# Maxima of an attention unit: four bursts of two pairs, or three bursts of 3, 2 and 3 over two-bank tiles, and VectorE's ramp order written out

## The chip, the cores and the metric

The kernel runs on one core of a Trainium2 chip. The metric is the time of one execution on the device in microseconds; the median of three runs before the change is 1043.43 us. TensorE (PE) with its weight loads (PEld), VectorE (DVE), ScalarE (ACT) and GpSimd (POOL) each work through their own queue in order; SyncE (SP) issues most DMAs, in order too.

## The reference

```python
xn = _layernorm(x)                                   # x: 1 x 2048 x 640
q, k, v = split(xn @ wqkv)                           # 32 heads of 20
scores = q @ k^T * 20 ** -0.5, masked to 0 <= i - j < 256
o = softmax(scores) @ v @ wo
h = gelu(xn @ w_gate) * (xn @ w_up)                  # 1728 wide
return x + o + h @ w_down
```

All is float32, and softmax subtracts each row's maximum.

## The kernel before

**Products.** Dense products are made of three passes over a high and a low half of each operand (`dense_steps`): `ps_d` for q, k, gate and up, `ps_v` for v. The normalized input, transposed, is held as `xh` and `xl` in four chunks of 512 tokens (`C`).

**Three stages.** The *ramp* (to about 88 us) loads x by tiles of 128 tokens (`xi`), normalizes them (`ln_stats`, `ln_sqrt`, `ln_rstd`, `ln_apply`), transposes them on PE (`ps_t`), splits them (`xh` on ScalarE, `xl` on VectorE) and makes the first projections. Then `attention()` runs to about 541 us. After it come the remaining gate and up products (`ps_g`) and the products with `w_down` and `wo` (`ps`); the change leaves both alone.

**Attention** works in units: one group of 4 heads and one chunk of 512 queries, 8 groups by 4 chunks, 32 units. Each unit's loop has 14 slots (`NS`). What a slot does is written in the order in which each engine shall run it: PE, ACT, DVE, POOL and SP all take the order of the code there. In a slot come, one after the other:
- what was put off to this slot (`at`, `defer`, run by `tick`), with `max_end` last;
- maxima for the *next* unit (`pull_max`, `max_pair`), in some slots;
- in slot 0 the products of the last unit's `P` with v (`av_unit`: `ps_o`, 96 matmuls, 64 for a first chunk; then the copies `ob` and `P` on ACT, and three slots later `ob + P` on POOL, `ob` L630);
- in odd slots up to 11 two score pieces and their exponentials (`exp_piece`: `ps_e`, `P`);
- what was kept for the slot's end (`late`, `flush`), and loads of `qs` and `ks` for the unit after the next two (`load_stack`, slots 9 and 12);
- some 2.2 matmuls of dense work, the *fill* (`pull_fill(RATE / NS)`): projections and gate and up products that don't depend on the unit.

**The maxima.** A unit has 8 *pairs*. One pair is 128 queries of two heads: PE writes the scores of 320 keys into two PSUM tiles (`ps_m`, one for each half of PE's rows) with matmuls of 64 by 64 that use the four quadrants of the array side by side (L512), and VectorE adds the mask and takes the maximum of each tile in one reduction (`junk`, L522), which a second instruction reads out into `mx`. After the eighth pair two small VectorE instructions (`negate`, L531 and L532) make the negated maxima `nm` in two bf16 parts, `late`, at the slot's end. `max_end` transposes them on PE (`ps_n`, L539), copies them (`mr`, ACT) and sends them by DMA into two rows of `qs`, from where the score pieces of the next unit subtract them. `max_end` comes `MXD` = 7 slots after the eighth pair.

A *burst* is the pairs of one `pull_max`. Before, bursts of two pairs stand in slots 0 (ahead of `av_unit`), 0 again (behind it; in slot 3 of the first unit), 5 and 9. PSUM's 8 banks are two for `ps_d`, `ps_v` (`psd`), two for `ps_e`, `ps_o` (`psx`) and four tiles of one bank each for `ps_m`, `ps_n` (`psm`), which are used in turn.

**Beside it.** POOL clears what the mask hides in `P` (L592, L595), subtracts the low halves of weights (`wql`, L661), of projections (`pt`, L259), and in slots 0 to 2 of units 2 to 28 makes sums of `x` (`tx`, L758) for the last stage. `save_qk` moves a projection out in three steps; `LAG` says how many slots ScalarE's second step comes after VectorE's.

Of the kernel before, what the change touches and what calls it, by code (L numbers as in the profile page):

```python
# [9 lines left out]
F32 = mybir.dt.float32  # L10
# [10 lines left out]
NC = S // C  # L21
# [46 lines left out]
def block_kernel(ctx, tc, x, wqk, wv, wgu, wdo, wdl, out):  # L68
# [71 lines left out]
    psm = pp.enter_context(tc.tile_pool(name="psm", bufs=4, space=PSUM))  # L140

    def ln_load(t, lp):
        xi = lp.tile([128, D], F32, name="xi", tag="xi", bufs=8)
# [24 lines left out]
    def ln_apply(xi, mv, rs):  # L168
        nc.vector.tensor_scalar(xi, xi, mv[:, 0:1], rs, op0=OP.subtract, op1=OP.mult)  # L169

    def ln_scale(xs, lp, mv=None, begun=0):
        n = len(xs)
        mv = mv or lp.tile([128, n, 2], F32, name="mv4", tag="mv4", bufs=2)
        for i in range(begun, n):
            ln_stats(xs[i], mv[:, i, :], lp)
        rs = ln_rstd(*ln_sqrt(mv, n, lp), n, lp)
        for i, xi in enumerate(xs):
            ln_apply(xi, mv[:, i, :], rs[:, i:i + 1])

    def turn(k, xs, where):  # L180
        n = len(xs)
        pool, tag = {"x": (psx, "ex"), "m": (psm, "mx"), "o": (psm, "mx")}[where]
        ps = pool.tile([128, n * 128], F32, name="ps_t", tag=tag)
        for i in range(n):
            nc.tensor.transpose(ps[:, i * 128:(i + 1) * 128], xs[i][:, k * 128:(k + 1) * 128], ident)  # L185
        return ps

    def ln_turn(t0, xs, where="xmxmx"):
        n = len(xs)
        cs = slice(t0 * 128, (t0 + n) * 128)  # L190
        for k in range(KT):
            ps = turn(k, xs, where[k])
            nc.scalar.activation(xh[:, k, cs], ps, AF.Copy)
            nc.vector.tensor_tensor(out=xl[:, k, cs], in0=ps, in1=xh[:, k, cs].bitcast(F32), op=OP.subtract)  # L194

    acts = {}
    done = set()
# [27 lines left out]
    def behind(fn, *a):  # L225
# [3 lines left out]
        else:  # L229
            fn(*a)  # L230

    def load_qk(t):
        raw = wrp.tile([128, KT, 128], F32, name="wr", tag="wr")
        nc.sync.dma_start(raw, wqk[t])
        return raw

    def split_qk(raw):
        return split(wp, raw, [128, KT, 128], "wq", nc.gpsimd)
# [106 lines left out]
    def first_chunk(xs, wr0, wr5, prep, v0, lp):  # L345
# [26 lines left out]
        with tc.manual_schedule(engines=MANUAL | {mybir.EngineType.Pool}):  # L372
# [53 lines left out]
                    pass  # L426
            for j in range(4):
                ln_apply(xs[4 + j], mv[:, j, :], rs[:, j:j + 1])
            save_qk(0, 0, dn[0])
            mv = lp.tile([128, 4, 2], F32, name="mv4", tag="mv4", bufs=2)  # L430
            for j in range(2):
                ln_stats(xs[8 + j], mv[:, j, :], lp)
        save_qk(5, 0, dn[1])
        return w0, w5, v0, mv

    v0 = []
    with tc.tile_pool(name="lp", bufs=1, side="right") as lp:
        xs = [ln_load(t, lp) for t in range(2)]
        wr0 = load_qk(0)
        xs += [ln_load(t, lp) for t in (2, 3)]  # L440
        wr5 = load_qk(5)
        warm = lp.tile([128, 256], BF, name="warm")[:, 0:128]
        nc.vector.memset(warm, 0.0)
        ps = psd.tile([128, C], F32, name="ps_u", tag="dn")
        for i, n in enumerate(WARM):
            if i:
# [6 lines left out]
        w0, w5, v0, mv = first_chunk(xs, wr0, wr5, prep, v0, lp)  # L453
        ones = lp.tile([4, 2 * C], BF, name="ones")
        nc.gpsimd.memset(ones, 0.0)
        nc.gpsimd.memset(ones[0:2], 1.0)
        for i in range(NK):
            for j in (0, 2):
                nc.sync.dma_start(ks[i][SR:64, j:j + 2].rearrange("p j t -> p (j t)"), ones)
        for c in range(1, NC):  # L460
            if c > 1:
                ln_scale(xs[4 * c:4 * c + 4], lp, *((mv, 2) if c == 2 else ()))
            ln_turn(4 * c, xs[4 * c:4 * c + 4], "xmxmx" if c == NC - 1 else "xmxmm")
            if 1 < c < NC - 1:
                xs += [ln_load(t, lp) for t in range(4 * c + 4, 4 * c + 8)]
            if c == 1:
                for i in range(NQ):
                    for j in (0, 2):
                        nc.sync.dma_start(qs[i][SR + 2:64, j:j + 2].rearrange("p j t -> p (j t)"), ones[2:4])
            if c == 2:  # L470
                raws1 = [load_qk(1), load_qk(6)]
            if c < NC - 1:
                run(*[proj_v(v0, 4 * c - 4 + i, None if i % 2 else (psm, "mx")) for i in range(0 if c > 1 else 2, 4)])
                run(proj_qk(0, w0, c), proj_qk(5, w5, c))
# [15 lines left out]

    maxes = {}

    def max_pair(u, i):
# [5 lines left out]
        pss = [psm.tile([128, 320], F32, name="ps_m", tag="mx") for _ in range(2)]  # L499
        n = 320 if c else min(320, 128 * b + 128)  # L500

        def quarters(cut):
            for h in range(2):
                part = cut(128 * b + 64 * h - 256, 128 * b + 64 * h + 64)
                for r, ps in enumerate(pss):
                    if part is not None:
                        kt, col, k0, k1 = part
                        rows, j = slice(64 * r, 64 * r + SR), 2 * r + jj
                        q0 = 128 * b + 64 * h
                        ks_ = kt[rows, j, 0:1].to_broadcast([SR, 64]) if k0 == k1 else kt[rows, j, k0:k1]  # L510
                        w = max(64, k1 - k0) if k0 == k1 else k1 - k0
                        nc.tensor.matmul(ps[64 * h:64 * h + 64, col:col + w], q[rows, j, q0:q0 + 64], ks_,  # L512
                                         start=True, stop=True, tile_position=(64 * r, 64 * h))
# [5 lines left out]
        quarters(lambda lo, hi: (k, max(0, -lo), max(0, lo), hi))  # L519
        junk = ap.tile([128, 320], BF, name="junk", tag="junk", bufs=1)  # L520
        for r, ps in enumerate(pss):
            nc.vector.tensor_tensor_reduce(out=junk[:, 0:n], in0=ps[:, 320 - n:320], in1=mask[:, 320 - n:320], scale=1.0,  # L522
                                           scalar=NEG, op0=OP.add, op1=OP.max,
                                           accum_out=maxes[u][:, 2 * r + jj, b:b + 1])
        if i == 7:
            mx = maxes.pop(u)
            nm = nms[u % 2]
            maxes[u] = nm

            def negate():  # L530
                nc.vector.tensor_scalar(nm[:, 0, 0], mx, -1.0, None, op0=OP.mult)  # L531
                nc.vector.scalar_tensor_tensor(nm[:, 0, 1], mx, -1.0, nm[:, 0, 0], op0=OP.mult, op1=OP.subtract)  # L532

            late(negate)
# [105 lines left out]
    def load_gu(f):  # L640
        raws = []
        for i in range(2 if f < NF - 1 else 1):
            raw = wrp.tile([128, KT, 128], F32, name="wr", tag="wr")
            nc.sync.dma_start(raw, wgu[2 * f + i])
            raws.append(raw)
        return raws

    def split_gu(pools, raws):
# [154 lines left out]
    debt = [0.0]  # L803

    def pull_max(n, slot):
        for _ in range(n):
            x = next(stream, None)
            if x is None:
                return
            max_pair(*x)  # L810
            if x[1] == 7:
                at(slot + (MXD if slot >= 0 else 4), max_end, x[0])

    def tick():
        todo = [y for t in sorted(t for t in acts if t <= now[0]) for y in acts.pop(t)]
# [7 lines left out]
    def attention():  # L823
# [8 lines left out]
        for i in range(12):  # L832
# [3 lines left out]
            if i == 0:  # L836
                pull_max(1, now[0])
                pull_fill(RAMP)
                pull_max(1, now[0])
                debt[0] -= RAMP  # L840
            elif i % 2 == 0:
                pull_max(2, now[0])
            flush()
            pull_fill(2 * RAMP)
        pull_fill(GAP)
        for u in range(NU + 1):
# [686 lines left out]
```

## Time and profile before

| | us |
|---|---|
| runs | 1042.8, 1043.43, 1046.78 |
| profiled execution | 1043.06 |
| its span, first to last instruction | 1041.3 |
| ramp / its last bursts / attention's units / the rest | 0 to 88 / to 101.4 / to 541 / to 1041 |
| granted TensorE clock | 1.000 throughout |

Rows of the profile have the line of the kernel, the engine, the operation, the tiles written and read, and either a count with busy time and mean duration or, in order of time, start and length in us. A matmul's length holds the time that it takes through the array, so that lengths overlap; starts are what tells the pace.

### The profile page before, as it was taken

The numbers are of one execution on the slowest core, as the hardware profiler recorded it, in microseconds if no ns is written. First come the engines' busy times: TensorE is split into PE (matmuls) and PEld (weight loads), VectorE is DVE, ScalarE is ACT, GpSimd is POOL, SyncE is SP. The second block draws the span as 40 slices with busy tenths as digits, with TensorE's granted clock in tenths as the row PEclk, the third lists the DMA queues.
The fourth block names the chain that finished last, engine by engine and source line by source line (L and its number), as shares of the span: only waits on it lengthen the run. The fifth ranks groups of instructions, "written<-read, shape, count | busy, mean of one in ns | idle before, by whom it ended". The sixth has DMA issues, their size and how long they took to land.

```text
span 1041.3 us, 25568 instructions
## 1 busy us (share of the span) xinstructions
PE 1031.8 (99%) x9396; PEld 834.4 (80%) x9396; DVE 740.3 (71%) x2018; ACT 527.9 (51%) x1120; POOL 384.5 (37%) x623
## 2 busy tenths in 40 slices
PE   9999999999999999999999999999999999999998
PEld 8887666666777666666678888888888999999998
DVE  7855666677656576777736778776556888888887
ACT  4434766767666666666675322223324544333332
POOL 5122778988765787766461111101110000000000
PEclk9999999999999999999999999999999999999999
DMA  6642356564633455343325576673117874433333
GB/s 224 182 144 70 110 157 182 160 181 142 185 98 99 117 150 163 94 145 109 99 76 190 187 248 212 246 256 110 72 58 268 252 244 138 137 128 111 127 122 105
DMA packets 102150, 158.74 MB, mean 152 GB/s; under 512 B 14172, under 2 KB 55260, under 8 KB 102024
## 3 DMA queue, kind: packets, MB, share of 16 engines
q1 hardware_dynamic: 99640, 150.94, 45.7%
q10 hardware_dynamic: 2384, 6.16, 1.9%
q8 instruction: 74, 1.21, 0.5%
q14 instruction: 52, 0.43, 0.1%
HBM read 101.78 MB, written 54.92 MB: 150 GB/s over the span
## 4 chain that ended last, share of the span: by engine, by line
PE 92%; DVE 5%; DMA 1%; issue 1%; ACT 1%; SPq 0%; DVEq 0%; ACTq 0%
PE ps_g L977 24%; PE ps L1249 23%; PE ps_d L108 19%; PE ps_e L577 8%; PE ps_v L108 6%; PE ps_o L620 5%; PE ps_m L512 5%; DVE junk L522 2%; PE ps_g L108 1%; PE ps_d L356 1%; DVE xi L169 0%; DMA qs<-qd 0%; PE ps_t L185 0%; DVE st L150 0%; DVE xl L194 0%
## 5 line engine op out<-in xcount | busy, mean ns | idle before, releaser
L522 DVE CUSTOM_DVE_ANT_0 junk<-ps_m,mask 128x320 bf16<-128x320 f32 (+2 forms) x512 | 242.5, 474 | 132.1 <-PE ps_m L512 73.6
L579 ACT ACTIVATE P<-ps_e 128x512 f32<-128x512 f32 (+2 forms) x384 | 198.7, 572 | 65.3 <-PE ps_e L577 64.6
L1249 PE MATMUL ps<-wb,at 128*128 128x320 f32 x999 | 155.9, 309 | 0.0
L1249 PEld LDWEIGHTS ps<-wb,at 128*128 128x128 f32 x999 | 148.9, 188 | 0.2
L592 POOL TENSOR_SCALAR_AFFINE_SELECT P<-P 128x256 f32<-128x256 f32 (+1 forms) x192 | 94.7, 495 | 72.4 <-ACT P L579 71.6
L577 PE MATMUL ps_e<-qs,ks 124*128 124x128 bf16 (+2 forms) x704 | 118.3, 278 | 0.1
L108 PE MATMUL ps_d<-xl,wqh 128*128 128x512 f32 x310 | 98.5, 421 | 0.0
L108 PE MATMUL ps_d<-xh,wqh 128*128 128x512 f32 x310 | 98.3, 421 | 0.0
L108 PE MATMUL ps_d<-xh,wql 128*128 128x512 f32 x310 | 97.6, 418 | 0.0
L101 POOL TENSOR_TENSOR wql<-wr,wqh 128x640 fp32r<-128x640 f32 x12 | 19.2, 1607 | 195.4 <-PE ps_g L977 150.8
L1249 PE MATMUL ps<-wt,at 128*128 128x320 f32 x552 | 88.9, 309 | 0.0
L577 PEld LDWEIGHTS <-ks 124*128 124x128 bf16 x704 | 49.5, 98 | 49.0 <-issue 34.4
L1249 PEld LDWEIGHTS ps<-wt,at 128*128 128x128 f32 x552 | 82.9, 188 | 0.1
L595 POOL TENSOR_SCALAR_AFFINE_SELECT P<-P 128x512 f32<-128x512 f32 (+1 forms) x144 | 76.8, 542 | 16.3 <-ACT P L579 16.3
L1203 ACT ACTIVATE at<-ss 128x512 fp32r<-128x512 f32 x59 | 37.3, 632 | 83.3 <-DVE ss L1082 83.3
L620 PE MATMUL ps_o<-P,v 64*32 64x320 f32 (+4 forms) x2816 | 74.2, 347 | 0.0
L259 POOL TENSOR_TENSOR pt<-r,pt 128x512 bf16<-128x512 f32 x40 | 46.7, 1167 | 64.4 <-ACT pt L255 64.0
L620 PEld LDWEIGHTS ps_o<-P,v 64*32 64x32 f32 x2816 | 50.8, 106 | 21.5 <-issue 0.9
L512 PE MATMUL ps_m<-ks,qs 60*64 60x320 bf16 (+3 forms) x1472 | 64.0, 260 | 3.2 <-DMA qs<-qd 1.1
L108 PEld LDWEIGHTS ps_d<-xh,wql 128*128 128x128 f32 x310 | 56.0, 189 | 10.2 <-issue 1.3
L1006 ACT ACTIVATE hr<-hr 128x512 f32<-128x512 f32 x20 | 12.6, 632 | 101.6 <-DVE hr L980 101.6
L108 PEld LDWEIGHTS ps_d<-xh,wqh 128*128 128x128 f32 x310 | 56.0, 189 | 9.8 <-issue 1.6
(197 smaller groups left out, 1981.6 us busy)
## 6 DMA issues: line engine op xcount, KB each, us to landing
hd<-he SPq DMA_DIRECT2D x50, 256.0 KB
hr<-hd SPq DMA_DIRECT2D x48, 256.0 KB
wr<-wgu SPq DMA_DIRECT2D x27, 320.0 KB
qs<-qd SPq DMA_DIRECT2D x64, 120.0 KB
ks<-kd SPq DMA_DIRECT2D x64, 120.0 KB
xi<-x SPq DMA_DIRECT2D x16, 320.0 KB
qs<-qd SPq DMA_DIRECT2D x64, 80.0 KB
ks<-kd SPq DMA_DIRECT2D x64, 80.0 KB
```

The source lines that it names most:

```text
L108: nc.tensor.matmul(ps, a(k), b(k), start=n == 0, stop=n == 3 * nk - 1)
L259: nc.gpsimd.tensor_tensor(out=pt[:, l, :], in0=r, in1=pt[:, 1, :], op=OP.subtract)
L512: nc.tensor.matmul(ps[64 * h:64 * h + 64, col:col + w], q[rows, j, q0:q0 + 64], ks_, start=True, stop=True, tile_position=(64 * r, 64 * h))
L522: nc.vector.tensor_tensor_reduce(out=junk[:, 0:n], in0=ps[:, 320 - n:320], in1=mask[:, 320 - n:320], scale=1.0, scalar=NEG, op0=OP.add, op ...
L577: nc.tensor.matmul(ps[:, col:col + n], k[0:QROWS, j, kc:kc + 128], q[0:QROWS, j, q0:q0 + n], start=True, stop=True)
L579: nc.scalar.activation(pt[:, j, lo:hi], ps[:, lo:hi], AF.Exp, scale=SCALE)
L592: nc.gpsimd.affine_select(out=a, in_=a, pattern=[[0, n], [1, 128]], compare_op=OP.is_ge, fill=0.0, base=0, channel_multiplier=-1)
L595: nc.gpsimd.affine_select(out=a, in_=a, pattern=[[0, n], [-1, 128]], compare_op=OP.is_ge, fill=0.0, base=-1, channel_multiplier=1)
L620: nc.tensor.matmul(os[r][32 * j:32 * j + 32, qa:qb], v[rows, w0_:w0_ + 32], pt[rows, j, col + qa - q0:col + qb - q0], start=r not in begun ...
L977: nc.tensor.matmul(ps, i, j, start=first and n == 0, stop=n == len(work) - 1, skip_group_check=True)
L1203: nc.scalar.activation(hi[:, 3:7], s, AF.Copy)
L1249: nc.tensor.matmul(ps[bank][:, 0:HD], *work[bank][j], start=bank not in begun, stop=final[p, bank] == n and j == len(work[bank]) - 1, skip ...
```

## The change

1. **Bursts.** From the first unit on, the four single-bank tiles are given up for two tiles of two banks (`widen`, `wide`), one for each half of PE's rows. A burst writes all its pairs into these two (`max_group`), at columns 0 and 512, or 0, 320 and 640; the middle pair of three crosses from one bank into the next, so `mul` cuts its matmuls in two. Of three pairs the third is reduced first, then the first and the second. Bursts of 3, 2 and 3 pairs stand in slots 0, 4 and 8 (`GROUPS`), none behind `av_unit`. One pair more than before is done ahead of the units, so that a unit's eighth pair falls into slot 0.
2. **`negate`** follows the burst's reductions at once, and `max_end` comes 2 slots later (`MXD`) in place of 7; `ps_n` lies in the first of the two tiles.
3. **Ramp.** VectorE's instructions of the chunks 1 to 3 run in the order of the code; a chunk's normalization is written behind the split of the one before, and the statistics of its first two tiles (`ln_begin`) earlier still.
4. **Loads of weights** that come in a slot after 4 are put off to the unit's last slot (`load_later`); `LAG` has other numbers.

The core of the diff:

```diff
-MXD = 7
+MXD = 2
+GROUPS = {0: 3, 4: 2, 8: 3}
-LAG = 3, 5, 4, 4, 4, 4, 3, 3, 4, 3, 2, 1, 1, 1
+LAG = 4, 5, 4, 4, 5, 4, 3, 3, 6, 5, 4, 3, 2, 1
...
+    def widen():
+        pm.close()
+        wide.append(pm.enter_context(tc.tile_pool(name="psw", bufs=1, space=PSUM, reuse_waits="tile")))
...
+    def load_later(src):
+        raw = wrp.tile([128, KT, 128], F32, name="wr", tag="wr")
+        i = 0 if now[0] is None or now[0] < 0 else now[0] % NS
+        if i > 4:
+            at(now[0] + NS - 1 - i, lambda: nc.sync.dma_start(raw, src))
+        else:
+            nc.sync.dma_start(raw, src)
+        return raw
...
-        for c in range(1, NC):
-            if c > 1:
-                ln_scale(xs[4 * c:4 * c + 4], lp, *((mv, 2) if c == 2 else ()))
-            ln_turn(4 * c, xs[4 * c:4 * c + 4], "xmxmx" if c == NC - 1 else "xmxmm")
...
+        with tc.manual_schedule(engines={mybir.EngineType.DVE}):
+            for c in range(1, NC):
+                ln_turn(4 * c, xs[4 * c:4 * c + 4], "xmxmd" if c == NC - 1 else "xmxmm",
+                        (lambda: save_qk(5, 0, k_first)) if c == 1 else None)
+                if c == NC - 1:
+                    break
+                ln_scale(xs[4 * c + 4:4 * c + 8], lp, mv)
...
+    BANK = 512
+    PLACES = {1: (0,), 2: (0, BANK), 3: (0, 320, 640)}
+
+    def max_group(pairs):
+        if wide:
+            both = [wide[0].tile([128, 2 * BANK], F32, name=f"ps_m{r}", tag=f"m{r}") for r in range(2)]
+            todo = [max_pair(u, i, both, base) for (u, i), base in zip(pairs, PLACES[len(pairs)])]
+        else:
+            todo = [max_pair(u, i, [psm.tile([128, 320], F32, name="ps_m", tag="mx") for _ in range(2)], 0)
+                    for u, i in pairs]
+        for n in (2, 0, 1) if len(pairs) == 3 else range(len(pairs)):
+            reduce_pair(*todo[n])
+        for u, i in pairs:
+            if i == 7:
+                negate(u)
...
+        def mul(ps, r, h, kt, col, k0, w):
+            rows, j, q0 = slice(64 * r, 64 * r + SR), 2 * r + jj, 128 * b + 64 * h
+            while w:
+                m = min(w, BANK - (base + col) % BANK)
+                ks_ = kt[rows, j, 0:1].to_broadcast([SR, m]) if k0 is None else kt[rows, j, k0:k0 + m]
+                nc.tensor.matmul(ps[64 * h:64 * h + 64, base + col:base + col + m], q[rows, j, q0:q0 + 64], ks_,
+                                 start=True, stop=True, tile_position=(64 * r, 64 * h))
+                col, w, k0 = col + m, w - m, k0 if k0 is None else k0 + m
...
-        ps = psm.tile([128, 128], F32, name="ps_n", tag="mx")
+        ps = wide[0].tile([128, 2 * BANK], F32, name="ps_n", tag="m0")[:, 0:128] if wide else psm.tile(
+            [128, 128], F32, name="ps_n", tag="mx")
...
-                if i in (0, 5, 9) or T == 3:
-                    pull_max(2, T)
+                if i in GROUPS:
+                    pull_max(GROUPS[i], T)
                 if i == 0 and u:
                     if u == NU:
                         pull_fill(LAST)
                     av_unit(u - 1)
                     flush()
-                    pull_max(2, T)
```

On PE behind `av_unit` of an ordinary unit, before: the last products with v, the burst of two pairs (each of 8 matmuls with a weight load of its own), then the fill.

```order
L620 MATMUL ps_o<-P,v 32x128 x8
L620 MATMUL ps_o<-P,v 32x64 x8
...
L512 MATMUL ps_m<-ks_182,qs_177 64x320
L512 LDWEIGHTS qs_177
L512 MATMUL ps_m<-ks_182,qs_177 64x320
...
```

The same place of a unit with the change (here v's projection is the fill, and `nm_183` holds the negated maxima):

```order
L664 MATMUL ps_o<-P,v 32x64 x4
L109 MATMUL ps_v<-wvl,xh_76 128x320 x3
L621 LDWEIGHTS ks_179
L621 MATMUL ps_e<-qs_177,ks_179 128x128
...
L109 MATMUL ps_v<-wvh,xh_76 128x320
L583 LDWEIGHTS nm_183
L583 MATMUL ps_n<-identb,nm_183 128x128
L109 MATMUL ps_v<-wvh,xh_76 128x320 x4
```

The burst behind `ps_o` has gone, and `ps_n` with its weight load of `nm` stands a few matmuls behind `ps_o`, ahead of slot 2's fill. The middle pair of a burst of three on PE, ahead of `av_unit`; `ps_m_4994` and `ps_m_4995` are the two wide tiles:

```order
L544 LDWEIGHTS qs_178
L544 MATMUL ps_m_4994<-ks_181,qs_178 64x192
L544 LDWEIGHTS qs_178
L544 MATMUL ps_m_4994<-ks_181,qs_178 64x128
L544 LDWEIGHTS qs_178
L544 MATMUL ps_m_4995<-ks_181,qs_178 64x192
L544 LDWEIGHTS qs_178
L544 MATMUL ps_m_4995<-ks_181,qs_178 64x128
```

What was one matmul of 320 columns is now two of 192 and 128, one right after the other in the same quadrant. VectorE's last reductions ahead of `nm`, with the engines that each instruction waits for, before:

```order
L522 ISA junk,mx<-ps_m,mask 128x320 [waits DVE_49,PE_49]
L522 ISA mx 128x1
L522 ISA junk,mx<-ps_m,mask 128x320 [waits DVE_49,PE_49]
L522 ISA mx 128x1
L531 TENSOR_SCALAR nm_183<-mx 128x16 [waits DVE_49]
L532 SCALAR_TENSOR_TENSOR nm_183<-mx,nm_183 128x16 [waits DVE_49]
```

And with the change, the six reductions of slot 0's burst:

```order
L569 ISA junk,mx<-ps_m_4994,mask 128x320 [waits DVE_49,PE_49]
L569 ISA mx 128x1
L569 ISA junk,mx<-ps_m_4995,mask 128x320 [waits DVE_49,PE_49]
L569 ISA mx 128x1
L569 ISA junk,mx<-ps_m_4994,mask 128x320 [waits DVE_49]
...
L569 ISA junk,mx<-ps_m_4995,mask 128x320 [waits DVE_49]
L569 ISA mx 128x1
L576 TENSOR_SCALAR nm_183<-mx 128x16 [waits DVE_49]
L577 SCALAR_TENSOR_TENSOR nm_183<-mx,nm_183 128x16 [waits DVE_49]
```

Only the first two of a burst wait for PE; the others wait for VectorE's own last instruction alone.

More of the change, by code (lines that the diff above doesn't have):

```diff
@@ L169, in ln_apply, with ln_begin, ln_scale @@
         nc.vector.tensor_scalar(xi, xi, mv[:, 0:1], rs, op0=OP.subtract, op1=OP.mult)
-    def ln_scale(xs, lp, mv=None, begun=0):
+    def ln_begin(xs, lp):
+        mv = lp.tile([128, 4, 2], F32, name="mv4", tag="mv4", bufs=2)
+        for i in range(2):
+            ln_stats(xs[i], mv[:, i, :], lp)
+        return mv
+    def ln_scale(xs, lp, mv):
         n = len(xs)
-        mv = mv or lp.tile([128, n, 2], F32, name="mv4", tag="mv4", bufs=2)
-        for i in range(begun, n):
+        for i in range(2, n):
             ln_stats(xs[i], mv[:, i, :], lp)
@@ L186, in turn, with ln_turn @@
         return ps
-    def ln_turn(t0, xs, where="xmxmx"):
+    def ln_turn(t0, xs, where, mid=None):
         n = len(xs)
@@ L194, in ln_turn @@
             nc.vector.tensor_tensor(out=xl[:, k, cs], in0=ps, in1=xh[:, k, cs].bitcast(F32), op=OP.subtract)
+            if k == 2 and mid:
+                mid()
     acts = {}
@@ L230, in behind @@
             fn(*a)
+    def load_later(src):
[6 more added lines that the diff above has]
+        return raw
     def load_qk(t):
[L233 to L235 removed]
+        return load_later(wqk[t])
     def split_qk(raw):
@@ L428, in first_chunk @@
                 ln_apply(xs[4 + j], mv[:, j, :], rs[:, j:j + 1])
+            mv = ln_begin(xs[8:], lp)
             save_qk(0, 0, dn[0])
[L430 to L434, printed above, removed]
+        return w0, w5, v0, mv, dn[1]
     v0 = []
@@ L507, in quarters @@
                         kt, col, k0, k1 = part
[L508 to L513, printed above, removed]
+                        if k0 == k1:
+                            mul(ps, r, h, kt, col, None, 64)
+                        else:
+                            mul(ps, r, h, kt, col, k0, k1 - k0)
         if c:
@@ L805, in pull_max @@
     def pull_max(n, slot):
[L806 to L812, printed above, removed]
+        pairs = [x for x in (next(stream, None) for _ in range(n)) if x]
+        if pairs:
+            max_group(pairs)
+        for u, i in pairs:
+            if i == 7:
+                at(slot + (MXD if slot >= 0 else 4), max_end, u)
     def tick():
```

62 lines of the change are left out of this document (31 added, 31 removed).

## Prediction, written before the changed kernel ran

> **What bounds the kernel now.** I read the page first, then the chain, the waits of PE, and PE's rows in order of time.
>
> ```profile
> span 1041.3 us, 25568 instructions
> PE 1031.8 (99%) x9396; PEld 834.4 (80%) x9396; DVE 740.3 (71%) x2018; ACT 527.9 (51%) x1120; POOL 384.5 (37%) x623
> ...
> PE 92%; DVE 5%; DMA 1%; issue 1%; ACT 1%; SPq 0%; DVEq 0%; ACTq 0%
> ```
>
> PE is busy for 99% of the span and carries 92% of the chain. So only two things shorten the run: work that PE no longer does, and moments in which PE really stands still. The stretches (busy time of PE, PEld, DVE, ACT, POOL in that order) and PE's own list of waits say how little of the second there is.
>
> ```profile
> 0.00:38.00 38.00, 35.86 (x257) 32.34 (x257) 30.58 (x94) 17.51 (x51) 17.54 (x38) 1.00 0.65 221
> 38.00:88.00 50.00, 49.06 (x329) 41.94 (x330) 27.86 (x84) 19.40 (x59) 10.24 (x9) 1.00 0.41 123
> ...
> 101.40:541.00 439.60, 436.97 (x5892) 298.45 (x5895) 288.35 (x1070) 295.73 (x647) 322.28 (x550) 1.00 0.45 133
> ```
>
> ```profile
> PE ps_t L185 <- DVE xi L169: 1.2, 3, 0.8
> ...
> PE ps_m L512 <- DMA qs<-qd: 1.1, 2, 0.6
> ```
>
> PE is idle for 2.1 + 0.9 us in the first 88 us and for 2.6 us in the attention units. These rows miss stalls shorter than a matmul's modelled tail, so I take starts of PE instructions, below. A unit of 14 slots takes 14.1 us (231.48 to 287.77 below is four units), so a slot is about 1 us; B is the start of a unit's first burst.
>
> **The change part by part.** First the burst behind the products with V (`ps_o`), which goes away. PE in an ordinary unit, and in the last but one, which has no bursts:
>
> ```profile
> 231.08 0.47 PE L512 MATMUL ps_m<-ks,qs 60*64 60x256 bf16 x16
> 231.48 2.45 PE L620 MATMUL ps_o<-P,v 64*32 64x320 f32 x96
> 233.85 0.47 PE L512 MATMUL ps_m<-ks,qs 60*64 60x320 bf16 x8
> 234.25 0.73 PE L108 MATMUL ps_d<-xl,wqh 128*128 128x512 f32 x2
> 234.82 0.40 PE L108 MATMUL ps_d<-xh,wqh 128*128 128x512 f32 x1
> 235.06 0.39 PE L577 MATMUL ps_e<-qs,ks 124*128 124x128 bf16 x2
> 235.15 0.53 PE L108 MATMUL ps_d<-xh,wqh 128*128 128x512 f32 x1
> 235.53 0.40 PE L577 MATMUL ps_e<-qs,ks 124*128 124x128 bf16 x2
> 235.62 1.00 PE L108 MATMUL ps_d<-xh,wqh 128*128 128x512 f32 x3
> ...
> 526.29 2.45 PE L620 MATMUL ps_o<-P,v 64*32 64x320 f32 x96
> 528.66 0.96 PE L108 MATMUL ps_d<-xl,wqh 128*128 128x512 f32 x3
> ```
>
> ```profile
> 800.95 237.08 PE ps L1249 x1615
> ```
>
> From `ps_o` to the next dense matmul it is 234.25 - 231.48 = 2.77 us with the burst and 528.66 - 526.29 = 2.37 without: the burst costs 0.40. Its two pairs are done elsewhere now. A pair streams 320 columns in each quadrant of the array, and 320 columns take 237.08 / 1615 = 0.147 us. So 0.40 - 2 x 0.147 = 0.106 us go, 30 units: **-3.2** (0 if every pair carries its share of the turn from one kind to the next, -6 if that turn costs twice as much).
>
> In the eight units whose `ps_o` is of a first chunk (64 matmuls) that burst also waits for VectorE to empty its tiles:
>
> ```profile
> 101.78 1.93 PE L620 MATMUL ps_o<-P,v 64*32 64x320 f32 x64
> 103.64 0.92 PE L512 MATMUL ps_m<-ks,qs 60*64 60x320 bf16 x8
> 104.50 0.73 PE L108 MATMUL ps_d<-xh,wql 128*128 128x512 f32 x2
> ```
>
> 0.86 in place of 0.40, so 8 x 0.46 = **-3.7** (none of it if VectorE holds PE up at the next place, which is the term on `ps_n` below).
>
> The middle pair of a burst of three crosses a bank, and its eight matmuls stand for four: 240 more in 60 pairs. Sixteen matmuls (231.08 to 231.48) and eight (233.85 to 234.25), both over 640 columns of each quadrant, took 0.40 us: the number alone costs nothing. But now both halves of one quadrant follow each other. If the second blocks the issue of the other quadrants, a pair takes twice its 0.147 us. Range 0 to +8.8; I take **+0.6**, near the row. The Trainium skill (TensorEngine Tiling, Performance Considerations) gives every matmul some 60 cycles of overhead; by it, with 25 ns a split pair as an estimate, the term would be +1.5 and the sum 0.9 more.
>
> VectorE's ramp order: PE's 1.2 us for `xi` may go: **-1.2** (from -3.0, all idle time of the first 88 us, to +2 if a written order puts something late, as long as one `xi` wait and its neighbours).
>
> Weight loads that come late in a unit are issued in its last slot, behind `qs` and `ks`. SP's queue before the one unit where PE waits for `qs`:
>
> ```profile
> 157.91 0.86 SPq L234 DMA_DIRECT2D wr<-wqk  x2
> ...
> 160.30 4.74 SPq L487 DMA_DIRECT2D qs<-qd  x6
> ```
>
> `qs` stood behind `wr`; that wait goes, **-1.1**. Against it the first pairs of a `qs` are needed one slot earlier: up to +3 (about 1 us in three units).
>
> Now `ps_n`, the transposition of the negated maxima: slot 2 in place of 7. All dense work is queued behind it on PE. When does PE reach it? A burst of three ends 0.40 + 0.147 = 0.55 after B, the next dense matmul comes 2.37 later, and of dense matmuls four or five stand ahead of `ps_n`: by the rows from 234.25 to 235.62 and the ones behind it 1.52 or 1.75 us. So at B + 4.44 or 4.67, and where `ps_o` has 64 matmuls (103.64 - 101.78 = 1.86) at 3.9 or 4.2. And when are the maxima there? VectorE:
>
> ```profile
> 231.46 0.49 DVE L522 CUSTOM_DVE_ANT_0 junk<-ps_m,mask 128x320 bf16<-128x320 f32 x1 [1.01 <-PE ps_m L512]
> 231.87 0.08 DVE L522 DVE_READ_ACCUMULATOR2_ANT mx<- 128x1 f32 x1
> 232.10 0.49 DVE L522 CUSTOM_DVE_ANT_0 junk<-ps_m,mask 128x320 bf16<-128x320 f32 x1
> ...
> 236.57 0.08 DVE L522 DVE_READ_ACCUMULATOR2_ANT mx<- 128x1 f32 x1
> 236.69 0.51 DVE L531 TENSOR_SCALAR nm<-mx 128x16 bf16<-128x16 f32 x1
> 237.23 1.22 DVE L532 SCALAR_TENSOR_TENSOR nm<-mx,nm 128x16 bf16<-128x16 f32 x1
> ...
> 292.98 0.17 DVE L531 TENSOR_SCALAR nm<-mx 128x16 bf16<-128x16 f32 x1
> 293.19 0.17 DVE L532 SCALAR_TENSOR_TENSOR nm<-mx,nm 128x16 bf16<-128x16 f32 x1
> ```
>
> A reduction starts 0.38 after its pair on PE (231.46 - 231.08), so the first of six at B + 0.38 + 2 x 0.147 = 0.67 (all three pairs must be done: pair three is reduced first). The pitch is 0.64 where a reduction waits for two engines (0.15 from 231.95 to 232.10), but `nm`, which waits for VectorE alone, came 0.04 after the accumulator (236.65 to 236.69). In the new order four of six wait for VectorE alone: pitch 0.53. Last accumulator at 0.67 + 0.64 + 4 x 0.53 + 0.50 = 3.93, first `nm` 3.97 to 4.14, second 4.18 to 4.35; PE can go on at 4.40. That is just in time for an ordinary unit, and 0.3 to 0.5 late in the eight. But GpSimd decides:
>
> ```profile
> 236.44 0.73 POOL L758 TENSOR_TENSOR tx<-tx,xl 128x256 f32<-128x256 f32 x1
> 237.12 1.29 POOL L630 TENSOR_TENSOR ob<-ob,P 128x512 f32<-128x512 f32 x1
> ...
> 287.37 0.47 PE L512 MATMUL ps_m<-ks,qs 60*64 60x256 bf16 x16
> 287.77 2.45 PE L620 MATMUL ps_o<-P,v 64*32 64x320 f32 x96
> ...
> 291.39 1.28 POOL L630 TENSOR_TENSOR ob<-ob,P 128x512 f32<-128x512 f32 x1 [1.04 <-ACT P L627]
> ...
> 104.90 1.16 POOL L630 TENSOR_TENSOR ob<-ob,P 128x448 f32<-128x448 f32 x1 [2.48 <-ACT P L627]
> ```
>
> Both `nm` of 0.17 us became 0.51 and 1.22, and ended within 0.04 of the end of `tx` (237.17) and of `ob` (238.41): a `nm` that finds such a GpSimd instruction begun waits for its end. In the eight units `ob` starts 104.90 - 101.78 = 3.12 after `ps_o`, so at B + 3.67, until 4.83: the second `nm` ends near 5.0 and PE stands for up to 1.1 us. Where `tx` keeps `ob` away it is 0.4. I take 0.75: 8 x 0.75 = 6.0. In the ordinary units `tx` and the weights' low halves meet the `nm` now and then as at 236.44; an estimate of five times 0.4 = 2.0. **+8.0** (0 if none is hit, 8 x 1.1 + 22 x 1.0 = +31 if all are).
>
> The tile that `ps_n` uses is the next burst's: its copy must be done within the 1.6 us (two slots) between them. ScalarE has the exponentials ahead of it: **+1.0** (0 to +5, 0.15 in each unit). The other reductions have 3 us and more from burst to burst for 2.4 or 3.3 us of work: nothing.
>
> Sum: -3.2 - 3.7 + 0.6 - 1.2 - 1.1 + 8.0 + 1.0 = +0.4. The profiled execution took 1043.06 us (1.8 outside its span), the median of three is 1043.43; **1043.5 us**, no change. 0.5% is 5.2 us, about what a measurement of this kernel can tell from none.
>
> **The rivals.** (1) *`ob` wins in the ordinary units: slower.* There it starts 291.39 - 287.77 = 3.62 after `ps_o`, at B + 4.17; the second `nm` wants to start at 4.18. If `ob` is first, that `nm` ends at 5.45 + 0.04 and PE stands for 0.85 to 1.05 us. Some ten units have no other GpSimd work ahead of `ob`: +10, **1053.5 us**. It decides from `nm` starting a few hundredths behind `ob`; for it speaks that 237.23 came 0.11 behind 237.12 and lost, against it that my 0.01 is smaller than the error of the sums. The Trainium skill (SBUF — State Buffer, SBUF: two separate sides) says that whichever of the two starts first holds the shared port pair for its whole instruction; by that rule, with my starts, the time is that of this rival; the row at 237.23 agrees.
> (2) *The `nm` get through: faster.* If GpSimd's work shifts so that `nm` meets none of it, only the eight units' 0.3 remain: 8.0 becomes 2.4 and the copy's 1.0 goes, 1043.5 - 6.6 = **1036.9 us**. For it: 292.98 and 293.19, unhindered as in most late units; against it: those came 5.6 us after their burst, when `ob` was past.
> (3) *The halves of a split pair block each other: slower,* 1043.5 + 8.2 = **1051.7 us**. Against it are the sixteen matmuls in 0.40 us.
>
> **How the numbers follow.** My sum 0.40, rival (1) 0.24, rival (2) 0.24, rival (3) 0.06, a new wait for `qs` or the copy at its upper bound 0.06 (1048.5 to 1050). Faster by over 0.5% (below 1038.2) is rival (2): 0.24; within, my sum: 0.40; slower the rest: 0.36. My sum's own range is 1038.5 to 1048.5. The range of 8 in 10 takes in both sides' centres: 1036 to 1055.
>
> **What would show it.** Three bursts a unit and none behind `ps_o`; reductions at a pitch near 0.53 within a burst; PE's or its weight load's wait for `nm` at `ps_n`, near 0.75 us in every fourth unit and none in most others (my sum), near 1 us in ten more (rival 1), nowhere above 0.4 (rival 2); a burst of three with 0.55 us to the next kind, or 0.7 (rival 3). Wrong altogether I would be if PE waited at the bursts of slots 4 and 8, or if the ramp moved by more than 3 us.

## The result, and the profile after

The changed kernel takes **1068.62 us** (median of four runs, 1067.61 to 1069.91); the kernel before takes 1043.12 us (four runs, 1041.68 to 1046.78). The ratio is 1.0243, 95% interval 1.0223 to 1.0262: 25.5 us slower, where the forecast was no change (1043.5, range 1036 to 1055). The profiled execution has a span of 1066.5 us against 1041.3.

The head of the page, after (span, busy time of each engine, the chain):

```profile
span 1066.5 us, 25749 instructions
PE 1040.1 (98%) x9640; PEld 834.4 (78%) x9640; DVE 758.1 (71%) x2018; ACT 531.3 (50%) x1120; POOL 382.2 (36%) x623
...
PE 84%; DVE 12%; ACT 1%; issue 1%; DMA 0%; SPq 0%; ACTq 0%; DVEq 0%
```

PE's share of the chain fell from 92% to 84%, VectorE's rose from 5% to 12%: there is a new place where PE stands for VectorE. The waits of PE and of its weight loads (us in total, times, longest) name it:

```profile
PE ps_n L583 <- DVE nm L577: 19.5, 25, 2.2
...
PE ps_t L197 <- DVE xi L176: 0.9, 3, 0.5
...
PEld L583 <- DVE nm L577: 29.4, 28, 2.5
```

Before, PE had no row at `ps_n`, and by the starts of its instructions it waited 0.0 us there. Taken from the starts of PE's instructions ("by starts" from here on; the row leaves out what lies under the modelled tail of the matmul before), PE stands 27.2 us at `ps_n`: 2.4 once ahead of the first unit and 24.8 in 30 units. The stretches (busy time of PE first) put the loss into the attention units, which now run from 102.6 to 565:

```profile
0.00:38.00 38.00, 35.77 (x261) 32.55 (x262) 32.30 (x94) 17.44 (x51) 17.52 (x38) 1.00 0.66 221
38.00:88.00 50.00, 49.82 (x341) 42.45 (x340) 28.01 (x88) 19.49 (x62) 10.21 (x9) 1.00 0.43 127
101.40:565.00 463.60, 445.11 (x6077) 297.89 (x6076) 303.51 (x1065) 299.45 (x648) 319.00 (x547) 1.00 0.43 126
```

The first `ps_o` starts at 102.58 in place of 101.78, and that includes the 2.4 us at `ps_n`, so the ramp by itself is some 1.6 shorter; the last `ps_o` starts at 564.99 in place of 539.77, 25.2 later; behind it both kernels take the same time.

An ordinary unit in order of time, from the burst of three (B = 297.66) to `ps_n`:

```profile
297.66 0.61 PE L544 MATMUL ps_m<-ks,qs 60*64 60x128 bf16 x20
...
298.19 2.45 PE L664 MATMUL ps_o<-P,v 64*32 64x320 f32 x96
298.31 0.49 DVE L569 CUSTOM_DVE_ANT_0 junk<-ps_m,mask 128x320 bf16<-128x320 f32 x1 [1.30 <-PE ps_m L544]
...
301.50 0.08 DVE L569 DVE_READ_ACCUMULATOR2_ANT mx<- 128x1 f32 x1
301.62 0.17 DVE L576 TENSOR_SCALAR nm<-mx 128x16 bf16<-128x16 f32 x1
...
301.81 1.27 POOL L674 TENSOR_TENSOR ob<-ob,P 128x512 f32<-128x512 f32 x1 [1.20 <-ACT P L671]
301.83 1.29 DVE L577 SCALAR_TENSOR_TENSOR nm<-mx,nm 128x16 bf16<-128x16 f32 x1
...
301.87 0.59 PE L109 MATMUL ps_v<-wvh,xh 128*128 128x320 f32 x2
...
303.18 0.23 PE L583 MATMUL ps_n<-identb,nm 128*128 128x128 bf16 x1 [0.72 <-DVE nm L577]
```

The first reduction starts at B + 0.65, the first `nm` at B + 3.96, GpSimd's `ob` at B + 4.15 and the second `nm` at B + 4.17, as the prediction's sums had it; `ob` is 0.02 ahead, the second `nm` takes 1.29 in place of 0.17 us and ends 0.04 behind `ob`, and PE, which had no more dense work ahead of `ps_n` from 302.30 on, goes on at 303.18. Thirteen ordinary units have `ob` begin within 0.13 us of the second `nm`. In ten of them `ob` is ahead, by 0.005 to 0.017 us, and each of these `nm` is held up. In the other three `nm` is ahead, by 0.12 us, and keeps its length:

```profile
316.86 0.17 DVE L577 SCALAR_TENSOR_TENSOR nm<-mx,nm 128x16 bf16<-128x16 f32 x1
316.98 1.28 POOL L674 TENSOR_TENSOR ob<-ob,P 128x512 f32<-128x512 f32 x1 [1.15 <-ACT P L671]
...
317.51 0.23 PE L583 MATMUL ps_n<-identb,nm 128*128 128x128 bf16 x1
```

In these three the burst is shorter (18 matmuls in place of 20), and the second `nm` starts at B + 4.01 in place of 4.17. In five of the eight units of a first chunk it's the first `nm` that meets `ob`:

```profile
105.69 1.14 POOL L674 TENSOR_TENSOR ob<-ob,P 128x448 f32<-128x448 f32 x1 [2.94 <-ACT P L671]
...
106.00 0.86 DVE L576 TENSOR_SCALAR nm<-mx 128x16 bf16<-128x16 f32 x1
...
106.89 0.17 DVE L577 SCALAR_TENSOR_TENSOR nm<-mx,nm 128x16 bf16<-128x16 f32 x1
...
107.12 0.23 PE L583 MATMUL ps_n<-identb,nm 128*128 128x128 bf16 x1 [0.78 <-DVE nm L577]
```

The 24.8 us by what GpSimd had running over an `nm`: `ob` in 20 units, 18.2 us (17 of them at 0.76 to 1.39, three where `nm` was ahead of it at 0 to 0.14); `pt` and `tx` of the x sums in 6 units, 4.6; `tx` or weight splits in 3, 1.8; nothing in one, 0.14. Not all of this is GpSimd's doing: in the units of a first chunk PE comes at B + 3.9 to 4.2, ahead of even an `nm` that nothing holds (one of the three with `tx`, where both `nm` took 0.17 us, still waits 0.42).

### The profile page after: what moved, and what is told of

Read it like the earlier page. It is cut to its first block, busy times and chain, and to the rows that moved or that the text cites. A ratio compares the mean times of both kernels' runs of the same rounds, so it can differ in the third digit from the quotient of the medians.

```text
span 1066.5 us, 25749 instructions
## 1 busy us (share of the span) xinstructions
PE 1040.1 (98%) x9640; PEld 834.4 (78%) x9640; DVE 758.1 (71%) x2018; ACT 531.3 (50%) x1120; POOL 382.2 (36%) x623
## 3 DMA queue, kind: packets, MB, share of 16 engines
HBM read 101.78 MB, written 54.92 MB: 147 GB/s over the span
## 4 chain that ended last, share of the span: by engine, by line
PE 84%; DVE 12%; ACT 1%; issue 1%; DMA 0%; SPq 0%; ACTq 0%; DVEq 0%
PE ps_g L1018 23%; PE ps L1290 22%; PE ps_d L109 18%; DVE junk L569 7%; PE ps_v L109 6%; PE ps_e L621 6%; PE ps_m L544 4%; DVE nm L577 2%; PE ps_g L109 1%; DVE nm L576 1%; PE ps_o L664 1%; PE ps_n L583 1%; PE ps_t L197 1%; ACT P L623 1%; PE ps_d L377 1%
## 5 line engine op out<-in xcount | busy, mean ns | idle before, releaser
L109 PE MATMUL ps_d<-xl,wqh 128*128 128x512 f32 x310 | 105.2, 430 | 0.0
L109 PE MATMUL ps_d<-xh,wqh 128*128 128x512 f32 x310 | 104.3, 429 | 0.0
L109 PE MATMUL ps_d<-xh,wql 128*128 128x512 f32 x310 | 102.9, 425 | 0.0
L639 POOL TENSOR_SCALAR_AFFINE_SELECT P<-P 128x512 f32<-128x512 f32 (+1 forms) x144 | 75.7, 534 | 16.1 <-ACT P L623 13.4
L109 PEld LDWEIGHTS ps_d<-xl,wqh 128*128 128x128 f32 x310 | 54.5, 189 | 8.7 <-issue 0.4
```

The source lines that it names most:

```text
L109: nc.tensor.matmul(ps, a(k), b(k), start=n == 0, stop=n == 3 * nk - 1)
L639: nc.gpsimd.affine_select(out=a, in_=a, pattern=[[0, n], [-1, 128]], compare_op=OP.is_ge, fill=0.0, base=-1, channel_multiplier=1)
```

## The experiments

Theory 1: the loss is PE standing behind `ps_n` for an `nm` that GpSimd holds up. Its first rival: bursts of three on two shared tiles hold PE up by themselves.

**`ps_n` at slot 6.**

```diff
-MXD = 2
+MXD = 6
```

> The changed kernel with one number altered: `ps_n` is queued on TensorE at slot 6 of a unit instead of slot 2; bursts, tiles, ramp and loads stay as changed. Theory 1 (the loss is TensorE standing behind `ps_n` while VectorE's second `nm` is held up by GpSimd's `ob` or `pt`): by slot 6 the `nm` have long been written, the 27 us of waits at `ps_n` fall under 1 us, and the time is about 1041.5 us, +-2, which is before less 1 to 2. Rival (bursts of three pairs on two shared tiles hold TensorE up themselves, since `ps_n` and the next burst take the tile that VectorE is still reading): the time stays above 1055 us and the wait shows up at another row.

Measured: 1055.8 us, 1.0129 times before (1.0115 to 1.0143). Far better than slot 2, but 14 us above what theory 1 gave. PE's waits and the place:

```profile
PE ps_n L583 <- DVE mx L569: 4.0, 14, 0.4
```

```profile
150.90 0.49 DVE L569 CUSTOM_DVE_ANT_0 junk<-ps_m,mask 128x320 bf16<-128x320 f32 x1 [1.13 <-PE ps_m L544]
...
152.07 0.49 DVE L569 CUSTOM_DVE_ANT_0 junk<-ps_m,mask 128x320 bf16<-128x320 f32 x1
152.49 0.08 DVE L569 DVE_READ_ACCUMULATOR2_ANT mx<- 128x1 f32 x1
...
152.63 0.23 PE L583 MATMUL ps_n<-identb,nm 128*128 128x128 bf16 x1 [0.41 <-DVE mx L569]
...
152.67 0.70 PE L109 MATMUL ps_d<-xh,wql 128*128 128x512 f32 x2
```

The wait for `nm` is gone and another has come: `ps_n` lies in the first wide tile, and PE stands until the third of the four reductions of slot 4's burst has read that tile (its accumulator is out at 152.57). By starts these waits are 7.9 us in all. So the rival's wait exists, at this slot and not at slot 2. Besides, `ps_n` stands alone between dense matmuls here; by starts PE's turns from one kind of matmul to another around it take some 4 us more in all than with `ps_n` right ahead of scores, at slot 7 (below), and the two together make up the 12 us by which slot 6 is slower than slot 7.

**`ps_n` at slot 3.**

```diff
-MXD = 2
+MXD = 3
```

> The changed kernel with `ps_n` queued at slot 3 in place of 2, one slot of scores and fill later (TensorE comes 0.5 to 0.7 us later). Theory 1: the second `nm` still ends at about 5.4 us after a unit's begin, so 0.3 to 0.7 of the 0.8 to 1.4 us of wait is left per unit: about 1055 us (1050 to 1060). If the wait had nothing to do with when TensorE arrives (a fixed cost of the tile or of `nm`), the time stays at 1068.

Measured: 1052.99 us, 1.0097 (1.0082 to 1.0113), as theory 1 had it. The wait shrinks as PE comes later and `nm` does not (11.3 us by starts, 9.5 of it in the units):

```profile
PE ps_n L583 <- DVE nm L577: 7.4, 18, 1.6
```

**`ob` two slots later.**

```diff
-        defer(3, join)
-        defer(6, store)
+        defer(5, join)
+        defer(8, store)
```

> The changed kernel with GpSimd's `ob` add put at slot 5 instead of 3 and its store at slot 8 instead of 6; `ps_n` stays at slot 2. Theory 1 (GpSimd's instruction that has begun holds VectorE's `nm` until it ends): in the ordinary units that have no other GpSimd work there, the wait at `ps_n` goes to about 0; in the first-chunk units it falls to about 0.35 us; where `pt` or `tx` of the x sums lie beside `nm`, it stays 0.5 to 1.1. Sum: about 1052 us (1047 to 1058). Rival (the second `nm` is slow on VectorE whatever GpSimd does, or TensorE waits for the reductions themselves): the time stays near 1068.

Measured: 1061.36 us, 1.018 (1.0167 to 1.0194). An ordinary unit now:

```profile
302.47 0.17 DVE L576 TENSOR_SCALAR nm<-mx 128x16 bf16<-128x16 f32 x1
...
302.68 0.18 DVE L577 SCALAR_TENSOR_TENSOR nm<-mx,nm 128x16 bf16<-128x16 f32 x1
...
303.15 0.23 PE L583 MATMUL ps_n<-identb,nm 128*128 128x128 bf16 x1
```

The second `nm` takes 0.18 and PE does not wait. By starts the waits at `ps_n` went from 27.2 to 12.2 us: 0 to 0.15 in the ordinary units without `pt`, 0.18 to 0.52 in those of first chunks, and still 0.49 to 1.15 in the six with `pt`. That is theory 1 as written, 15 us against 16. The time itself missed its range, because 8.4 us came back elsewhere in this execution: 3.3 us of PE's waits for `qs` at the bursts (by starts), 2.4 more ahead of scores, 0.9 inside the last `ps_o`, where GpSimd's masks come behind `ob`, 0.5 behind the units, and 1.3 ahead of the first `ps_o`, where the granted clock was 0.87:

```profile
88.00:101.40 13.40, 11.18 (x111) 8.74 (x111) 7.08 (x29) 7.64 (x24) 3.02 (x4) 0.87 0.22 67
```

What made the clock lower there stays open, and which of these come from `ob` and which from its store was not tried.

**The ramp alone**, put into the kernel before.

```diff
+        with tc.manual_schedule(engines={mybir.EngineType.DVE}):
+            for c in range(1, NC):
+                ln_turn(4 * c, xs[4 * c:4 * c + 4], "xmxmd" if c == NC - 1 else "xmxmm",
+                        (lambda: save_qk(5, 0, k_first)) if c == 1 else None)
...
+                if c == 1:
+                    mv = ln_begin(xs[12:], lp)
```

> The kernel before with the ramp part of the change alone: VectorE's order there written out, the row sums of a chunk begun a chunk earlier, the last transposes in `psd`. Theory: the ramp is shorter by 1.2 to 1.6 us as in the changed kernel's trace and nothing else moves: about 1042 us (1041 to 1043). Rival: written out order without the new bursts costs VectorE waits, +2 us.

Measured: 1041.61 us, 0.9995 (0.9985 to 1.0004), 0.7 less in the medians and not told apart from none. In its trace the first `ps_o` starts at 100.64 in place of 101.78, so the ramp is 1.1 shorter there. It has no part in the loss.

**`ps_n` back at slot 7**, all else as changed.

```diff
-MXD = 2
+MXD = 7
```

> The changed kernel with `ps_n` back at slot 7, as before the change; bursts of 3, 2 and 3, the two tiles, ramp and loads stay as changed. The run at slot 6 showed that there `ps_n` waits for VectorE to have read the burst of slot 4 out of the same tile (7.9 us in all, tile free at 8.1 to 8.6 us after a unit's begin), and that between dense matmuls, not next to scores, it costs some 0.1 to 0.2 us more a unit. At slot 7 TensorE comes about 1 us later than at slot 6 and goes on to scores. Theory 2 (`ps_n`'s place alone makes the loss: too early it meets `nm`, at 6 the tile): no wait at `ps_n`, about 1043 us (1041 to 1046). Rival: the burst of slot 8 then waits for ScalarE's `mr` to have read the tile, 0.3 to 0.6 us a unit: 1052 to 1060.

Measured: 1043.89 us, 1.0015 (1.0007 to 1.0024). One number gives back all but 1.3 of the 25.5 us. The `nm` are held up as they were with `ps_n` at slot 2; PE just isn't there yet:

```profile
291.03 1.28 POOL L674 TENSOR_TENSOR ob<-ob,P 128x512 f32<-128x512 f32 x1 [1.19 <-DMA td<-tx]
291.04 1.30 DVE L577 SCALAR_TENSOR_TENSOR nm<-mx,nm 128x16 bf16<-128x16 f32 x1
...
295.70 0.10 PEld L583 LDWEIGHTS <-nm 128*128 128x128 bf16 x1
295.71 0.23 PE L583 MATMUL ps_n<-identb,nm 128*128 128x128 bf16 x1
```

```profile
PE ps_m L544 <- DMA qs<-qd: 0.9, 1, 0.9
...
PE ps_m L544 <- ACT mr L585: 0.3, 1, 0.3
```

No row of PE at `ps_n` is left, and the rival, a wait of slot 8's burst for `mr`, occurs once, 0.3 us.

**The kernel before with `ps_n` at slot 2.**

```diff
-MXD = 7
+MXD = 2
```

> The kernel before with one number altered: `ps_n` at slot 2 instead of 7; four bursts of two and their four tiles stay. There `nm` ends 5.8 to 6.2 us after a unit's begin (its last two pairs come behind `ps_o`), and TensorE comes to slot 2 at about 4.4 to 4.9. Theory 2 (the place of `ps_n`, not the bursts): 1.0 to 1.4 us of wait in each of 31 units, about 1077 us (1070 to 1085), more than the changed kernel. If it's the bursts or the shared tiles that hold TensorE: under 1050 us.

Measured: 1100.25 us, 1.0552 (1.0538 to 1.0567).

```profile
PE ps_n L539 <- DVE nm L532: 43.3, 31, 2.4
```

```profile
334.81 0.17 DVE L531 TENSOR_SCALAR nm<-mx 128x16 bf16<-128x16 f32 x1
335.01 0.17 DVE L532 SCALAR_TENSOR_TENSOR nm<-mx,nm 128x16 bf16<-128x16 f32 x1
...
335.25 0.23 PE L539 MATMUL ps_n<-identb,nm 128*128 128x128 bf16 x1 [1.13 <-DVE nm L532]
```

By starts the waits are 51.4 us, 1.1 to 2.8 in each unit; I had expected 1.0 to 1.4. In 22 of the 30 units both `nm` take 0.17 us, as above: what is late there is the reductions of the two pairs behind `ps_o`, not an `nm` held by GpSimd. In the other eight GpSimd's work makes an `nm` longer too. With the two numbers in a table: old bursts 1042.6 at slot 7 and 1100.3 at slot 2; new bursts 1043.9 and 1068.6. The place of `ps_n` makes the loss, and the new bursts make that place cheaper (their `nm` mostly come 0.5 to 1.7 us sooner), not dearer.

**The old table LAG**, with `ps_n` at slot 7.

```diff
-LAG = 4, 5, 4, 4, 5, 4, 3, 3, 6, 5, 4, 3, 2, 1
+LAG = 3, 5, 4, 4, 4, 4, 3, 3, 4, 3, 2, 1, 1, 1
```

> As the first of these (`ps_n` at slot 7, bursts of 3, 2 and 3), with the table LAG as before the change, so that the steps of the weight splits and x sums on GpSimd and ScalarE stand in the slots they had. Theory 2: nothing waits for them when `ps_n` is late, so the same as the first within 2 us. Rival: the old table was fitted to the old bursts, or the new one costs scores their exponentials; then it is 3 us or more away, in either direction.

Measured: 1046.27 us, 1.0036 (1.0022 to 1.005): 2.4 us more than with the new table, just over the 2 that I gave theory 2. By starts the units have 3.3 us more of small waits, half of them at scores for the exponentials. The new table helps a little.

**Fill ahead of the first scores.** With slot 7 the units still took 2.8 us longer than before in the trace (of an execution of 1045.97 us, 2.1 above the median), though the burst behind `ps_o` is gone. By starts 3.9 us of that are new waits: the first scores of a unit come when ScalarE hasn't yet copied `ps_o` out.

```diff
                     if i == 1 and u:
                         pull_fill(1)
                         debt[0] -= 1
                     exp_piece(u, i - 1)
```

(these three lines added once more, ahead of the first scores)

> As the one before (`ps_n` at slot 7), with one step of dense fill taken from later and put ahead of a unit's first scores, so that ScalarE has freed `ps_o` when TensorE comes to `ps_e`. In the changed kernel the scores behind the attention-value matmuls wait 0.15 to 0.24 us in 22 units for that (about 4 us in all; before, a burst of two pairs stood there). Theory: 3 to 4 us less than with `ps_n` at slot 7 alone, 1039 to 1040 us if that one gives 1043. Rival: the fill that is missing later leaves the following scores waiting for ScalarE's exponentials, no gain.

Measured: 1044.85 us, 1.002 (1.0011 to 1.0029). Neither: each loan takes the step that the next would have given, so the fill between the two scores went away, and the wait moved to the second (3.9 us by starts). With one step ahead of each:

```diff
                     if i == 1 and u:
+                        pull_fill(1)
+                    exp_piece(u, i - 1)
+                    if i == 1 and u:
                         pull_fill(1)
-                        debt[0] -= 1
+                        debt[0] -= 2
```

> As `ps_n` at slot 7 with bursts of 3, 2 and 3 at slots 0, 4 and 8, with one step of dense fill ahead of each of a unit's first two scores, both borrowed from later (the earlier try put a step ahead of the first and took it from between the two, and the wait moved to the second). Theory: the first scores find both banks freed by ScalarE, 3 to 4 us of waits go, and 1 of them comes back as waits for exponentials later: about 1041 us. Rival: what is borrowed is missing between later scores, which then wait for the exponentials: 1043 to 1045.

Measured: 1043.56 us, 1.0003 (0.9993 to 1.0012). The waits for `ps_o` to be copied are gone, those of scores for exponentials rose from 2.2 to 5.4 us by starts: the rival. In both places that were tried it is ScalarE that those scores wait for.

**Bursts next to scores.** Theory 3: at slots 4 and 8 a burst stands alone in the dense stream and pays for a turn to its kind and back which slots 5 and 9 shared with the scores.

```diff
-GROUPS = {0: 3, 4: 2, 8: 3}
+GROUPS = {0: 3, 5: 2, 9: 3}
```

(with `ps_n` at slot 7)

> The changed kernel with `ps_n` at slot 7 and the bursts of two and three at slots 5 and 9 in place of 4 and 8, so that each stands right ahead of scores, as two of the four did before the change. With `ps_n` at slot 7 the units took 2.8 us longer than before, all together, though the burst behind `ps_o` and VectorE's waits there were gone. Theory 3: at slots 4 and 8 a burst stands alone between dense matmuls and pays for a turn to its kind and back that it shared with the scores before; back at odd slots 58 bursts save some 0.05 us each: 1041 us (1040 to 1042.5). Rival: the turns cost the same anywhere, no difference from 1043.9; or `ps_n` at slot 7 now meets VectorE still reading slot 5's burst out of its tile (0.1 to 0.5 us a unit): 1047 to 1058.

Measured: 1048.75 us, 1.0049 (1.0037 to 1.0062). The rival: `ps_n` at slot 7 meets VectorE at slot 5's burst, in the same tile.

```profile
PE ps_n L583 <- DVE mx L569: 7.9, 19, 0.9
```

That row leaves out what lies under the modelled tails; by starts PE waits 11.9 us at `ps_n` here. Against slots 4 and 8 the time is only 4.4 longer (each against its own run of before), so something was gained as well. There, the dense matmuls between one of the 58 bursts and the next scores took 0.10 us more, by starts, than their columns do, 6.0 us in all; with the bursts at 5 and 9 the scores follow at once, and this is gone. Theory 3 has its saving here, and the tile costs more.

Together with the two steps of fill it's no better:

> Bursts at slots 0, 5 and 9, `ps_n` at slot 7, and the two borrowed steps of fill ahead of the first scores, together. If both theories hold: about 1038.5 us, under the kernel before by 4; if the tile holds `ps_n` up at slot 7, over 1044.

Measured: 1048.1 us, 1.0044 (1.0031 to 1.0056), with the same row of 7.9 us. And with slot 3 in place of 5:

```diff
-GROUPS = {0: 3, 4: 2, 8: 3}
+GROUPS = {0: 3, 3: 2, 9: 3}
```

> As the one before, with the burst of two at slot 3 instead of 5, so that VectorE has read its tile long before `ps_n` at slot 7. Theory 3: the shared turn is kept and nothing waits: 1041 us. Rival: at slot 3 the burst meets VectorE still reducing slot 0's three pairs out of the same tiles (these end 4 us after a unit's begin, TensorE comes at about 5): some 0.1 to 0.5 us a unit, 1045 to 1055.

Measured: **1041.27 us**, 0.9973 (0.996 to 0.9986): in the medians 1.8 us under the kernel before, which ran at 1043.03 beside it, and 27 under the changed one; the fastest of all here. The ramp alone, not told apart from none, had given 0.7. The burst of three in the two kernels, PE from the start of the five dense matmuls around or ahead of it. At slot 8 (`ps_n` at 7):

```profile
310.98 0.45 PE L109 MATMUL ps_v<-wvl,xh 128*128 128x320 f32 x2
311.36 0.61 PE L544 MATMUL ps_m<-ks,qs 60*64 60x320 bf16 x20
311.89 0.71 PE L109 MATMUL ps_v<-wvl,xh 128*128 128x320 f32 x3
312.44 0.61 PE L621 MATMUL ps_e<-qs,ks 124*128 124x128 bf16 x4
312.75 1.04 PE L109 MATMUL ps_v<-wvh,xh 128*128 128x320 f32 x5
```

At slot 9:

```profile
312.10 0.89 PE L109 MATMUL ps_v<-wvl,xh 128*128 128x320 f32 x5
312.92 0.61 PE L544 MATMUL ps_m<-ks,qs 60*64 60x320 bf16 x20
313.46 0.61 PE L621 MATMUL ps_e<-qs,ks 124*128 124x128 bf16 x4
313.77 0.45 PE L109 MATMUL ps_v<-wvh,xh 128*128 128x320 f32 x1
```

The same work takes 312.75 - 310.98 = 1.77 us apart and 313.77 - 312.10 = 1.67 side by side: 0.10 a burst, by 58 bursts 5.8, in line with the 6.0 by starts. The medians, each against its own run of before, differ by 3.1. Some of the rest are new waits, since the pairs of slot 3 need their `qs` a slot sooner:

```profile
PE ps_m L544 <- DMA qs<-qd: 3.0, 3, 1.8
```

But that profiled execution took 1043.94 us, 2.7 more than the median, so this row is not typical of the median.

## Why the prediction was wrong, step by step

- **`ps_n`, +8.0 (0 to +31): the step that failed.** It measured 27.2 by starts, near the upper end that I had worked out and not taken. Its parts were right to a few hundredths: the first `nm` at B + 3.96 (3.97 to 4.14 in the prediction), `ob` at 4.15 (4.17), PE at the fill's end at 4.4 to 4.8 (4.44 to 4.67). The mechanism, an `nm` that waits for the end of a GpSimd instruction, was right. What failed is its size, by the choice of the middle: the ordinary units were set at 5 x 0.4, though my own starts had `ob` 0.01 ahead of the second `nm`. Of the 22 ordinary units 18 waited 0.4 to 1.15 us, 16.1 in all in place of 2.0; the eight of first chunks 8.7 in place of 6.0 (the 0.3 to 0.5 us that they'd wait for VectorE alone come out of the prediction's sums as 0.2 to 0.5; with `ob` moved away they waited 0.18 to 0.52); and 2.4 came at a `ps_n` ahead of the units, which I hadn't costed.
- **Rival (1)** is what happened, in place, price (0.76 to 1.13 a unit) and deciding point; I gave it ten units at 1.0, and `ob` won in ten, 9.75 us. Its 1053.5 is still 15 short, since the x sums and weight splits held PE up in eight more (6.1 in place of 2.0), by the 2.7 and 2.4 just named, and by the two terms that follow. The Trainium skill's rule that the one which starts first holds the shared port pair for its whole instruction (SBUF — State Buffer, SBUF: two separate sides) agrees with the trace: 0.02 us of lead cost 1.12 us of an instruction of 0.17, and with `ob` moved away it took 0.18. I let the error of my sums outweigh it; but 0.01 either way was an even chance at 10 us, not a reason to price it at near nothing. Nor is the chance drawn anew in each unit: units of one kind repeat their times to about 0.01 us, so that `ob` won each of these ten.
- **The burst behind `ps_o`, -3.2; right, but a term was missing beside it.** The burst is gone, and by starts the time in all bursts, waits left out, fell from 45.8 to 41.9 us. Not in my sum: the bursts of slots 5 and 9 stood right ahead of scores, and at 4 and 8 they stand alone. The rows make that 58 x 0.10 = +5.8, and slots 3 and 9 got 3.1 of it back in the time. With this and the next point the bursts gain nothing as placed (1.0015 with `ps_n` at slot 7).
- **Scores behind `ps_o`: missing too.** The burst that was removed had filled PE's time while ScalarE copied `ps_o`; without it the first scores wait, +3.4 us by starts in the changed kernel. I had asked what is late next only for VectorE.
- **VectorE's waits in first-chunk units, -3.7:** by starts the burst behind `ps_o` waited 0.45 us in each of the eight before, 3.6 in all, and no burst waits so in the changed kernel. Right.
- **Split pair, +0.6 (0 to +8.8):** the burst of three takes 298.19 - 297.66 = 0.53 us to the next kind, 0.54 in most units, where 0.40 + 0.147 = 0.55 was worked out with the cut free of cost. By starts the next matmul of a quadrant comes 0.08 us after the half of 192 columns and 0.06 after that of 128, 0.14 together, and 0.16 after an uncut one of 320. Rival (3) is out. So is the +1.5 by the 60 cycles a matmul of the Trainium skill (TensorEngine Tiling (Array Packing), Performance Considerations): in these starts the cut adds no time.
- **Ramp, -1.2:** 1.6 shorter in the changed kernel's trace, 1.1 alone. Right in size, below what the times can tell; the mechanism is shown in part only. PE's row for `xi` fell from 1.2 to 0.9 us and its idle time from 38 to 88 us from 0.94 to 0.18; where the rest comes from stays open.
- **Weight loads behind `qs`, -1.1:** waits at the bursts went from 1.3 to 0 by starts, 0.8 came at scores; with slot 7 they are back at 1.3. Nothing to speak of.
- **The tile of `ps_n`, +1.0:** the copy `mr` holds nothing up (one 0.3). But the tile was a cost in the other direction that I hadn't seen: at slot 6, and at slot 7 with a burst at slot 5, `ps_n` itself waits for VectorE to have read the tile, rows of 4.0 and 7.9 us, 7.9 and 11.9 by starts.

Added up, the measured terms come to some 27 us; the last `ps_o` comes 25.2 later and the medians are 25.5 apart, so no large term is missing.

"Wrong altogether if PE waited at the bursts of slots 4 and 8" did not occur.

## What to carry to other kernels

When an operation is moved earlier in an in-order queue, set the time of its last operand beside the time at which the queue gets there, unit by unit; where the two race within the error of the sums, price the lost race in all those units, since one outcome can repeat in each of them, as it did in ten here. A delay on a side engine may stand in every trace for long and cost nothing (an `nm` of 1.30 us at slot 7); it is the consumer's slot that makes it a bound. And when work is moved or removed on PE, look at its neighbours: what kind it stood beside, and what it gave another engine time for.

## What the runs showed of the hardware

- 0.02 us decides 1.1 us: a VectorE instruction of 0.17 us that began 0.005 to 0.02 behind a GpSimd `tensor_tensor` of 1.27 ended some 0.04 behind its end, in ten units; in three in which it began 0.12 ahead it kept its 0.17.
- A burst of 12 to 20 matmuls of 60 rows costs 0.10 us more alone between fp32 matmuls than right ahead of bf16 scores (1.77 against 1.67 us for the same work), and cutting a matmul of 320 columns into 192 and 128 costs nothing that can be seen (0.54 us for three pairs).
